# Attention over a cache on one core: row sums ahead of the values, the output weights spread around the last V blocks, and the result stored in halves

## The chip, the cores and the metric

The kernel runs on one core of a Trainium2 chip. The metric is the device time of one execution in microseconds (us). All durations that are read from a profile come from one profiled execution.

## The reference

Eight sequences of four tokens each (32 tokens) attend over a cache of 2048 keys and values. There are 32 query heads and 8 key/value heads of width 128, so four query heads share one key/value head.

```python
q = (x @ wq).reshape(B, Sq, Hq, Dh).transpose(0, 2, 1, 3)     # B=8, Sq=4, Hq=32, Dh=128
k = jnp.repeat(k_cache, 4, axis=1)                            # k_cache: (8, 8, 2048, 128) bf16
v = jnp.repeat(v_cache, 4, axis=1)
scores = jnp.einsum("bhqd,bhkd->bhqk", q, k) * (Dh ** -0.5)
p = softmax(scores, axis=-1)
o = jnp.einsum("bhqk,bhkd->bhqd", p, v)
return o.transpose(0, 2, 1, 3).reshape(B, Sq, Hq * Dh) @ wo   # wo: (4096, 512) bf16
```

The caches are 32 MB each, and wq and wo are 4 MB each.

## The kernel before

**Units and steps.** The work is cut into 32 units. A unit is one pair p of key/value heads (p = 0 to 3) of one sequence b (b = 0 to 7), with p as the outer index. Each unit has a K block and a V block of 1 MB each. Each unit is worked on in two half steps (hf = 0 and 1), so there are 64 half steps. The order of the instructions on each engine is the order in which the program writes them (a manual schedule), and the framework adds the waits.

**One pass of the main loop (L316).** The K side runs ahead of the V side. In the pass with number `step`, half step i = step + 7 has its K block transposed on TensorE (`transpose_part`, L199) and copied out of PSUM to `kt`. VectorE (DVE) makes three of four such copies (L206) and ScalarE (ACT) the one for the second part of the second half (L204). Half step j = step + 6 has its scores computed (L217), and ACT writes their exponentials to `probs` (L227). Half step `step` itself has its values computed (`values`, 16 matmuls at L241 into `o_ps`).

**Row sums.** `norms(u)` multiplies the exponentials of a whole unit by a matrix of ones, in two matmuls into `l_ps` (L255). DVE sums the result over 16 chunks (L263) and takes the reciprocal (L267). In the kernel before, this stands ahead of the values of the unit's second half. `finish(u)` multiplies the values by the reciprocals (L272) into `oT_all`, behind the values of the second half.

**Back to token rows.** When the 8 units of a pair p are finished, `to_tokens(p)` transposes its 8 heads into `nat` (L284), and DVE copies them to `nat_sb` (L290). `to_wo_rows(p)` transposes these again in another order into `perm` (L299), and DVE copies them to `oP[p]` (L304). The two run in the even passes of the next pair with b = 1 and b = 2, and for the last pair behind the loop. `l_ps`, `nat` and `perm` share one PSUM buffer (pool `psum_l`).

**The output projection.** `project(p, r0, n)` adds n matmuls of 512 columns to `out_ps` (L308), with a part of wo as the moving operand. All 32 matmuls of the kernel accumulate into this one tile of 32 x 512 fp32. Project(0) runs in the pass NH - 5 = 59, and the others run behind the loop.

**The loads.** All loads are issued by SyncE (SP) on one queue, in the order of the list `loads` (L114 to L121): K blocks run three units ahead of V blocks, with wo quarter 0 behind V29. A K block waits for one of 7 buffers and a V block for one of 6 (`load_ready`, L123). In the pass NH - 1 - 2 * VB = 51 the list is empty, and the remaining quarters of wo are issued, the last of them in three pieces (L339 to L343). The end of the order of loads is thus V29, wo 0, V30, V31, wo 1, wo 2, wo 3 (4 + 2 + 2 rows). wo takes the SBUF space of wq.

**The end.** DVE and ACT each copy half of `out_ps` to `out_sb`, and SP stores it (L356 to L358).

Of the kernel before, what the change touches and what calls it, by code (L numbers as in the profile page):

```python
# [8 lines left out]
BF16 = mybir.dt.bfloat16  # L9
# [5 lines left out]
def kernel(  # L15
# [9 lines left out]
    nc = tc.nc  # L25

    B, Sq, D = x.shape
# [4 lines left out]
    T = B * Sq  # L32
# [7 lines left out]
    NU = G2 * B  # L40
    NH = 2 * NU
# [4 lines left out]
    WR = HP  # L46
    DH = D // 2
# [5 lines left out]
    const = ctx.enter_context(tc.tile_pool(name="const", bufs=1))  # L53
# [20 lines left out]
    pick = const.tile([128, 2, 2, Dh // 2], BF16, name="pick")  # L74
    ident4 = const.tile([128, 128], FP32, name="ident4")
    oT_all = const.tile([128, Hq, B, Sq], BF16, name="oT_all")
    out_sb = const.tile([T, D], BF16, name="out_sb")
    oP = [const.tile([128, WR, T], BF16, name=f"oP{p}") for p in range(G2)]
    ident = const.tile([128, 128], BF16, name="ident")
    ones = const.tile([128, 128], BF16, name="ones")  # L80
# [26 lines left out]
    def load_wo(p, r0, n):  # L107
        rows = wo[p * HP * 128 : (p + 1) * HP * 128, :].rearrange("(q r) j -> q r j", r=WR)
        nc.sync.dma_start(wo_sb[:, p, r0 : r0 + n, :], rows[:, r0 : r0 + n, :])
# [3 lines left out]
    loads = []  # L113
    for u in range(NU + KA):  # L114
        if u < NU:
            loads.append(("k", u))
        if u >= KA - 1 and u - KA + 1 < NU:
            loads.append(("v", u - KA + 1))
        if u == NU:
            loads.append(("wo", 0))  # L120
    loads.reverse()  # L121

    def load_ready(nk, nv):  # L123
# [16 lines left out]
    for e in range(2):  # L140
        for g in range(2):
            nc.vector.tensor_copy(
                out=pick[:, e, g, :], in_=ident[:, :].rearrange("d (k e) -> d e k", e=2)[:, e, :]
# [12 lines left out]
    for p in range(G2):  # L156
        psq = psum_s.tile([128, HP, T], FP32, tag="s", name="psq")
        for h in range(HP):
# [10 lines left out]
            out=qT_all[:, p, :, :, :],  # L169
            in_=psq[:, :, :].rearrange("d h (b s) -> d b h s", b=B),  # L170
            mul=scale,
        )
    for p in range(G2):
# [9 lines left out]
        for g in range(2):  # L183
            rows = slice(g * 64, (g + 1) * 64)
            (nc.scalar.copy if g else nc.vector.tensor_copy)(  # L185
                out=q_bd[rows, p, :, :, g, :], in_=pse[rows, :, :, :]
# [5 lines left out]
    def transpose_part(i, part):  # L192
        u, hf = divmod(i, 2)
        c0 = hf * HC + part * (HC // 2)
        kp = psum_k.tile([128, HC // 4, 128], FP32, tag="k", name="kp")
        k4 = ks[u][:, :, :].rearrange("s c d -> s (c d)").bitcast(FP32)
        for j in range(HC // 4):
            w = (c0 // 2 + j) * 128
            nc.tensor.transpose(kp[:, j, :], k4[:, w : w + 128], ident4[:, :])  # L199
        kp2 = kp[:, :, :].rearrange("k j s -> k (j s)").bitcast(BF16)  # L200
        k_t = ktpool.tile([128, HC // 4, 128, 2], BF16, tag="kt", name="kt")
        kt2 = k_t[:, :, :, :].rearrange("k j s e -> k (j s e)")
        if part == 1 and hf == 1:
            nc.scalar.copy(out=kt2, in_=kp2)  # L204
        else:
            nc.vector.tensor_copy(out=kt2, in_=kp2)  # L206
        kt[(i, part)] = k_t

    def scores(i):
        u, hf = divmod(i, 2)  # L210
        p, b = units[u]
        pr = probs[u % len(probs)]
        s_ps = psum_s.tile([128, HC, NQ], FP32, tag="s", name="s_ps")
        for j in range(HC // 2):
            k_t = kt[(i, j // (HC // 4))]
            for e in range(2):
                nc.tensor.matmul(  # L217
                    s_ps[:, 2 * j : 2 * j + 2, :],
                    lhsT=k_t[:, j % (HC // 4), :, e],
                    rhs=q_bd[:, p, e, b, :, :],  # L220
                    start=(e == 0),
                    stop=(e == 1),
                )
        for g in range(2):
            rows = slice(g * 64, (g + 1) * 64)
            cols = slice(g * NQ // 2, (g + 1) * NQ // 2)
            nc.scalar.activation(  # L227
                out=pr[rows, hf * HC : (hf + 1) * HC, cols], in_=s_ps[rows, :, cols], func=EXP
            )
# [3 lines left out]
    def values(i):  # L233
        u, hf = divmod(i, 2)
        p, b = units[u]
        pr = probs[u % len(probs)]
        if hf == 0:
            o_ps[u] = psum_o.tile([128, NQ], FP32, tag="o", name="o_ps")
        for c in range(HC):
            cc = hf * HC + c  # L240
            nc.tensor.matmul(  # L241
                o_ps[u][:, :],
                lhsT=vs[u][:, cc, :],
                rhs=pr[:, cc, :],
                start=(cc == 0),
                stop=(cc == C - 1),
            )
# [3 lines left out]
    def norms(u):  # L251
        pr = probs[u % len(probs)]
        l_ps = psum_l.tile([128, LC, NQ], FP32, tag="l", name="l_ps")
        for c in range(0, C, LC):
            nc.tensor.matmul(  # L255
                l_ps[:, :, :],
                lhsT=ones[:, :],
                rhs=pr[:, c : c + LC, :],
                start=(c == 0),
                stop=(c + LC == C),  # L260
            )
        l_sb = small.tile([128, NQ], FP32, tag="l_sb", name="l_sb")
        nc.vector.tensor_reduce(  # L263
            out=l_sb[:, :], in_=l_ps[:, :, :].rearrange("d c q -> d q c"), axis=AX, op=ADD
        )
        r_sb = small.tile([128, NQ], FP32, tag="r_sb", name="r_sb")
        nc.vector.reciprocal(r_sb[:, :], l_sb[:, :])  # L267
        r_sbs[u] = r_sb

    def finish(u):  # L270
        p, b = units[u]
        nc.vector.tensor_tensor(  # L272
            out=oT_all[:, p * HP : (p + 1) * HP, b, :],
            in0=o_ps[u][:, :].rearrange("d (h s) -> d h s", h=HP),
            in1=r_sbs[u][:, :].rearrange("d (h s) -> d h s", h=HP),
            op=mybir.AluOpType.mult,
        )
# [3 lines left out]
    def to_tokens(p):  # L281
        nat = psum_l.tile([T, HP, 128], BF16, tag="l", name="nat")
        for h in range(HP):
            nc.tensor.transpose(  # L284
                nat[:, h, :],
                oT_all[:, p * HP + h, :, :].rearrange("d b s -> d (b s)"),
                ident[:, :],
            )
        nat_sb = small.tile([T, HP * 128 // WR, WR], BF16, tag="nat_sb", name="nat_sb")
        nc.vector.tensor_copy(  # L290
            out=nat_sb[:, :, :].rearrange("t q r -> t (q r)"),
            in_=nat[:, :, :].rearrange("t h d -> t (h d)"),
        )
        nats[p] = nat_sb

    def to_wo_rows(p):
        perm = psum_l.tile([128, WR, T], BF16, tag="l", name="perm")
        for r in range(WR):
            nc.tensor.transpose(  # L299
                perm[:, r, :],  # L300
                nats[p][:, :, :].rearrange("t q r -> t r q")[:, r, :],
                ident[:T, :T],
            )
        nc.vector.tensor_copy(out=oP[p][:, :, :], in_=perm[:, :, :])  # L304

    def project(p, r0, n):
        for r in range(r0, r0 + n):
            nc.tensor.matmul(  # L308
                out_ps[:, :],
                lhsT=oP[p][:, r, :],  # L310
                rhs=wo_sb[:, p, r, :],
                start=(p == 0 and r == 0),
                stop=(p == G2 - 1 and r == WR - 1),
            )

    for step in range(-L - 1, NH):  # L316
        i, j = step + L + 1, step + L
        if i < NH:
            transpose_part(i, 0)
        if 0 <= j < NH:  # L320
            scores(j)
        if i < NH:
            transpose_part(i, 1)
        u, hf = divmod(step, 2)
        if step >= 0:
            p, b = units[u]
            if hf == 1:
                norms(u)
            values(step)
            if hf == 1:  # L330
                finish(u)
            elif p > 0 and b == 1:
                to_tokens(p - 1)
            elif p > 0 and b == 2:
                to_wo_rows(p - 1)
        load_ready(min((i + 1) // 2, NU), max((step + 1) // 2, 0))
        if step == NH - 1 - 2 * VB:
            assert not loads
            load_wo(1, 0, WR)  # L339
            load_wo(2, 0, WR)  # L340
            load_wo(3, 0, 4)
            load_wo(3, 4, 2)
            load_wo(3, 6, 2)  # L343
        if step == NH - 5:
            out_ps = psum_s.tile([T, D], FP32, tag="s", name="out_ps")
            project(0, 0, WR)

    to_tokens(3)
    project(1, 0, 4)
    to_wo_rows(3)  # L350
    project(1, 4, 4)
    project(2, 0, WR)
    project(3, 0, 4)
    project(3, 4, 2)
    project(3, 6, 2)
    nc.vector.tensor_copy(out=out_sb[:, :DH], in_=out_ps[:, :DH])  # L356
    nc.scalar.copy(out=out_sb[:, DH:], in_=out_ps[:, DH:])  # L357
    nc.sync.dma_start(out=out.flatten_outer_dims(), in_=out_sb[:, :])  # L358


# [28 lines left out]
```

## Time and profile before

| | us |
|---|---|
| median of 6 runs | 193.42 |
| lowest and highest | 193.12, 194.64 |
| the profiled execution | 193.26 |
| its span on the core | 191.5 |

| engine | busy us (share of the span) |
|---|---|
| PE (TensorE matmul) | 153.6 (80%) |
| DVE (VectorE) | 112.5 (59%) |
| ACT (ScalarE) | 86.3 (45%) |
| queue of SP's loads | 95.3% of 16 DMA engines, 75.57 MB |

The profile's times count from the start of the span. PE is TensorE's matmuls, PEld its loads of weights, SPq the issuing of DMAs on SP. A row of the timeline gives the start, the duration from first to last, the engine, the line of the kernel, the operation, what it writes and reads, and how many instructions were merged; brackets give the idle time before it and what ended it. The chain of waits follows the work that ended last back to what released it at each step. TensorE's granted clock was at its full value throughout (1.0).

### The profile page before, as it was taken

Reading aid. Unit: us, or ns where it says so; the run is one execution under the profiler, and the core shown is the slowest. Engines: PE = TensorE matmul, PEld = TensorE weight load, DVE = VectorE, ACT = ScalarE, POOL = GpSimd, SP = SyncE. Lnnn points to the kernel's source line nnn. Section 1 sums busy time; section 2 is a strip of 40 time slices with the busy share of each in tenths; the row PEclk is TensorE's granted clock in tenths of the full one; section 3 lists DMA queues with packets and bytes.
Section 4 is the critical chain, followed back from the end, with each engine's and each line's share of the span. In section 5 each row is a group of like instructions: output and inputs, shape, how many; then the busy total and the mean of one; then the engine's idle time right before and its main releaser. Section 6 shows DMA issues by size and latency. Waiting matters only on the chain.

```text
span 191.5 us, 6364 instructions
## 1 busy us (share of the span) xinstructions
PE 153.6 (80%) x2830; PEld 136.0 (71%) x2860; DVE 112.5 (59%) x220; ACT 86.3 (45%) x170; POOL 1.1 (1%) x8
## 2 busy tenths in 40 slices
PE   0018977899999999999988889988885899889593
PEld 0016966788888888998888878877775788775451
DVE  6402754477776767777666667666663676665520
ACT  2004465655555555555554445444554455551000
POOL 2000000000000000000000000000000000000000
PEclk9999999999999999999999999999999999999999
DMA  6989999999999999999999999999999999999940
GB/s 226 438 368 430 419 426 414 419 423 418 418 419 419 418 419 418 421 419 414 428 412 421 421 414 424 414 423 416 421 416 423 418 423 418 412 428 414 401 170 7
DMA packets 10347, 75.97 MB, mean 397 GB/s; under 512 B 1168, under 2 KB 1232, under 8 KB 1616
## 3 DMA queue, kind: packets, MB, share of 16 engines
q1 hardware_dynamic: 10320, 75.57, 95.3%
q8 instruction: 22, 0.36, 0.8%
q14 instruction: 5, 0.04, 0.1%
HBM read 75.53 MB, written 0.03 MB: 395 GB/s over the span
## 4 chain that ended last, share of the span: by engine, by line
DMA 92%; PE 5%; DVE 1%; issue 0%; SPq 0%; ACT 0%; DVEq 0%
DMA k_sb<-in_k_cache_dram 64%; DMA v_sb<-in_v_cache_dram 21%; DMA wq_sb<-in_wq_dram 6%; PE out_ps L308 3%; PE kp L199 1%; PE o_ps L241 1%; PE l_ps L255 0%; DVE l_sb L263 0%; PE nat L284 0%; PE perm L299 0%; PE s_ps L217 0%; DVE out_sb L356 0%; SPq L111 0%; DVE r_sb L267 0%; ACT out_sb L357 0%
## 5 line engine op out<-in xcount | busy, mean ns | idle before, releaser
L206 DVE COPY kt<-kp 128x1024 bf16<-128x1024 bf16 x96 | 65.8, 688 | 44.8 <-PE kp L199 44.5
L199 PE MATMUL kp<-ident,k_sb 128*128 128x128 f32 x512 | 80.8, 284 | 10.1 <-DMA k_sb<-in_k_cache_dram 9.5
L227 ACT ACTIVATE probs<-s_ps 64x256 bf16<-64x256 f32 x128 | 48.4, 378 | 70.3 <-PE s_ps L217 69.5
L199 PEld LDWEIGHTS kp<-ident,k_sb 128*128 128x128 f32 x512 | 55.2, 143 | 11.7 <-issue 10.3
L217 PE MATMUL s_ps<-q_bd,kt 128*128 128x64 bf16 x1024 | 43.5, 193 | 6.7 <-ACT kt L204 6.0
L217 PEld LDWEIGHTS <-kt 128*128 128x128 bf16 x1024 | 39.6, 98 | 9.7 <-ACT kt L204 7.9
L241 PEld LDWEIGHTS <-v_sb 128*128 128x128 bf16 x1024 | 34.6, 96 | 10.0 <-DMA v_sb<-in_v_cache_dram 2.1
L241 PE MATMUL o_ps<-probs,v_sb 128*128 128x32 bf16 x1024 | 35.4, 176 | 1.7 <-DMA v_sb<-in_v_cache_dram 1.2
L204 ACT COPY kt<-kp 128x1024 bf16<-128x1024 bf16 x32 | 32.4, 1012 | 0.8
L263 DVE TENSOR_REDUCE l_sb<-l_ps 128x32 f32<-128x512 f32 x32 | 21.8, 682 | 5.0 <-remote 2.0
L255 PE MATMUL l_ps<-probs,ones 128*128 128x512 bf16 x34 | 12.6, 379 | 1.2
L267 DVE RECIPROCAL r_sb<-l_sb 128x32 f32<-128x32 f32 x32 | 11.3, 353 | 1.1
L185 DVE CAST q_bd<-pse 64x512 bf16<-64x512 f32 x4 | 2.6, 683 | 10.8 <-PE pse L176 10.8
L161 PE MATMUL psq<-xT_sb,wq_sb 128*128 128x32 bf16 x128 | 3.6, 188 | 6.3 <-DMA wq_sb<-in_wq_dram 6.3
L272 DVE TENSOR_TENSOR oT_all<-o_ps,r_sb 128x32 bf16<-128x32 f32 x32 | 6.1, 192 | 3.3
L161 PEld LDWEIGHTS <-wq_sb 128*128 128x128 bf16 x128 | 3.5, 104 | 6.4 <-DMA wq_sb<-in_wq_dram 6.4
L168 ACT ACTIVATE qT_all<-psq 128x256 bf16<-128x256 f32 x4 | 1.5, 386 | 14.0 <-PE psq L161 14.0
L308 PE MATMUL out_ps<-wo_sb,oP 128*32 128x512 bf16 x32 | 7.4, 380 | 0.0
L357 ACT CAST out_sb<-out_ps 32x256 bf16<-32x256 f32 x1 | 0.4, 362 | 15.3 <-DVE out_sb L356 15.3
L255 PEld LDWEIGHTS <-ones 128*128 128x128 bf16 x64 | 6.0, 98 | 0.4
L152 PE MATMUL xtp<-ident,x_sb 32*128 32x32 bf16 x4 | 0.5, 190 | 6.8 <-DVE xT_sb L155 4.3
L152 PEld LDWEIGHTS <-x_sb 32*128 32x128 bf16 x4 | 0.3, 112 | 6.8 <-issue 4.4
(23 smaller groups left out, 30.1 us busy)
## 6 DMA issues: line engine op xcount, KB each, us to landing
k_sb<-in_k_cache_dram SPq DMA_DIRECT2D x32, 1024.0 KB, 19.9
v_sb<-in_v_cache_dram SPq DMA_DIRECT2D x32, 1024.0 KB, 19.8
wq_sb<-in_wq_dram SPq DMA_DIRECT2D x1, 4096.0 KB, 12.4
wo_sb<-in_wo_dram SPq DMA_DIRECT2D x3, 1024.0 KB, 19.8
wo_sb<-in_wo_dram SPq DMA_DIRECT2D x1, 512.0 KB, 18.6
wo_sb<-in_wo_dram SPq DMA_DIRECT2D x2, 256.0 KB, 15.8
x_sb<-in_x_dram SPq DMA_DIRECT2D x1, 32.0 KB, 1.6
out_dram<-out_sb SPq DMA_DIRECT2D x1, 32.0 KB, 1.5
```

What stands on the lines that cost most here:

```text
L161: nc.tensor.matmul(psq[:, h, :], lhsT=wq_sb[:, r, hh * 128 : (hh + 1) * 128], rhs=xT_sb[:, r, :], start=(r == 0), stop=(r == R - 1),)
L199: nc.tensor.transpose(kp[:, j, :], k4[:, w : w + 128], ident4[:, :])
L204: nc.scalar.copy(out=kt2, in_=kp2)
L206: nc.vector.tensor_copy(out=kt2, in_=kp2)
L217: nc.tensor.matmul(s_ps[:, 2 * j : 2 * j + 2, :], lhsT=k_t[:, j % (HC // 4), :, e], rhs=q_bd[:, p, e, b, :, :], start=(e == 0), stop=(e == 1),
L227: nc.scalar.activation(out=pr[rows, hf * HC : (hf + 1) * HC, cols], in_=s_ps[rows, :, cols], func=EXP)
L241: nc.tensor.matmul(o_ps[u][:, :], lhsT=vs[u][:, cc, :], rhs=pr[:, cc, :], start=(cc == 0), stop=(cc == C - 1),)
L255: nc.tensor.matmul(l_ps[:, :, :], lhsT=ones[:, :], rhs=pr[:, c : c + LC, :], start=(c == 0), stop=(c + LC == C),)
L263: nc.vector.tensor_reduce(out=l_sb[:, :], in_=l_ps[:, :, :].rearrange("d c q -> d q c"), axis=AX, op=ADD)
L267: nc.vector.reciprocal(r_sb[:, :], l_sb[:, :])
L272: nc.vector.tensor_tensor(out=oT_all[:, p * HP : (p + 1) * HP, b, :], in0=o_ps[u][:, :].rearrange("d (h s) -> d h s", h=HP), in1=r_sbs[u][ ...
L308: nc.tensor.matmul(out_ps[:, :], lhsT=oP[p][:, r, :], rhs=wo_sb[:, p, r, :], start=(p == 0 and r == 0), stop=(p == G2 - 1 and r == WR - 1),)
```

## The change

Three things change. `norms(u)` moves from the unit's second half step to its first, ahead of the values of both halves. wo quarter 1 enters the list of loads behind V30, so the end of the order of loads becomes V29, wo 0, V30, wo 1, V31, wo 2, wo 3 in three pieces; project(1) moves into the pass NH - 3 = 61, behind the values of V30's second half. `out_sb` becomes two tiles of 256 columns, filled by DVE and ACT, and stored by a DMA of SP and one of ACT.

```diff
-    out_sb = const.tile([T, D], BF16, name="out_sb")
+    out_sb = [const.tile([T, DH], BF16, name=f"out_sb{i}") for i in range(2)]
...
-        if u == NU:
-            loads.append(("wo", 0))
+        if u in (NU, NU + 1):
+            loads.append(("wo", u - NU))
...
         if step >= 0:
             p, b = units[u]
-            if hf == 1:
+            if hf == 0:
                 norms(u)
             values(step)
...
         if step == NH - 1 - 2 * VB:
             assert not loads
-            load_wo(1, 0, WR)
             load_wo(2, 0, WR)
             load_wo(3, 0, 4)
             load_wo(3, 4, 2)
...
         if step == NH - 5:
             out_ps = psum_s.tile([T, D], FP32, tag="s", name="out_ps")
             project(0, 0, WR)
+        elif step == NH - 3:
+            project(1, 0, WR)
 
     to_tokens(3)
-    project(1, 0, 4)
     to_wo_rows(3)
-    project(1, 4, 4)
     project(2, 0, WR)
...
-    nc.vector.tensor_copy(out=out_sb[:, :DH], in_=out_ps[:, :DH])
-    nc.scalar.copy(out=out_sb[:, DH:], in_=out_ps[:, DH:])
-    nc.sync.dma_start(out=out.flatten_outer_dims(), in_=out_sb[:, :])
+    o2 = out.flatten_outer_dims()
+    nc.vector.tensor_copy(out=out_sb[0][:, :], in_=out_ps[:, :DH])
+    nc.scalar.copy(out=out_sb[1][:, :], in_=out_ps[:, DH:])
+    nc.sync.dma_start(out=o2[:, :DH], in_=out_sb[0][:, :])
+    nc.scalar.dma_start(out=o2[:, DH:], in_=out_sb[1][:, :])
```

## The prediction

> **What bounds the kernel now.** I read the page's chain of work first. DMA is 92% of it:
>
> ```profile
> DMA 92%; PE 5%; DVE 1%; issue 0%; SPq 0%; ACT 0%; DVEq 0%
> ```
>
> So until the last block lands, the engines follow the stream of loads. TensorE's own slack confirms it: in a middle step it sits 0.83 us before the K transposes, released by the load of K.
>
> ```profile
> 100.88 0.42 PEld L199 LDWEIGHTS kp<-ident,k_sb 128*128 128x128 f32 x4 [0.83 <-issue]
> 100.91 0.63 PE L199 MATMUL kp<-ident,k_sb 128*128 128x128 f32 x4 [0.76 <-DMA k_sb<-in_k_cache_dram]
> ```
>
> Next, the chain of waits in order of time, from 159 us on (start, duration, what):
>
> ```profile
> 159.45 19.78 DMA v_sb<-in_v_cache_dram
> 179.23 0.05 issue
> 179.28 0.57 PE o_ps L241 x16
> 179.84 0.45 PE l_ps L255 x2
> 180.30 0.02 issue
> 180.32 0.70 DVE l_sb L263
> 181.02 0.02 issue
> 181.04 0.36 DVE r_sb L267
> ...
> 181.50 0.20 DVE oT_all L272
> 181.70 0.04 issue
> 181.75 0.62 PE nat L284 x8
> 182.37 0.86 PE out_ps L308 x4
> 183.23 0.60 PE perm L299 x8
> 183.84 4.43 PE out_ps L308 x20
> ```
>
> After it come only the DVE copy (188.29 to 188.71), the ACT copy (188.74 to 189.10) and the store. From the landing of V31 at 179.23 to the last matmul at 188.27 is 9.04 us. The stream does not end there: three MB of wo follow. SP's own timeline gives each issue:
>
> ```profile
> 154.44 0.33 SPq L109 DMA_DIRECT2D wo_sb<-in_wo_dram  x1
> 156.98 2.80 SPq L102 DMA_DIRECT2D v_sb<-in_v_cache_dram  x2
> 161.89 10.25 SPq L109 DMA_DIRECT2D wo_sb<-in_wo_dram  x5
> 189.13 0.35 SPq L358 DMA_DIRECT2D out_dram<-out_sb  x1
> ```
>
> These are wo quarter 0, then V30 (156.98) and V31 (159.45), then quarters 1 to 3 in five pieces. Each MB lands 19.8 us after its issue, and issues are 2.47 us apart, since SP waits for a landing before each. So quarter 0 lands at 174.24, V30 at 176.76, V31 at 179.23, quarter 1 at 161.89 + 19.8 = 181.69. Taken issue by issue, the remaining pieces land at 184.2, 185.4, 186.0 and 186.7. TensorE reaches the first matmul on quarter 2 at 183.84 + 4 x 0.216 = 184.7 and on quarter 3 at 186.4. It waits for none: 20 matmuls in 4.43 us is an unbroken run. The end is therefore V31's landing plus TensorE's serial tail.
>
> [...] the ACT copy started 0.03 us after DVE's had ended. But both wrote one tile, out_sb[...]
>
> **The change, part by part**, against the profiled run (193.26 us, span 191.5, 1.76 around it; it lies 0.16 below the median of 193.42).
>
> 1. *wo.* Quarter 1 now leaves SP ahead of V31. Both are 1 MB in 8 KB runs, so the stream keeps its sizes and order and two labels change place: quarter 1 takes the landing at 179.23, V31 that at 181.69. **Cost +2.46 us** at the head of the tail. SP's 0.33 us of issue is only moved, and SP idles between issues. V31's buffer was free by 159.45, so it is at 161.89. Quarters 2 and 3 keep their landings.
>
> 2. *project(1) into the stream.* Its 8 matmuls now follow values(61). Quarter 1 is there at 179.23, so they run 179.28 to 181.01 in issue (8 x 0.216). They fill TensorE's wait for V31. This removes 8 matmuls from the tail, but not all at full price. The four between nat and perm took 0.86 us, and beside them ran DVE's copy of nat (0.68, plus 0.11 of handing over), on which perm waits anyway: saved 0.86 - 0.79 = 0.07. The four behind perm were bare: 4 x 0.216 = 0.87. **Together -0.94.**
>
> 3. *Row sums of unit 31.* Their 2 matmuls now stand behind project(1) and ahead of values(62). They finish at 181.01 + 0.60 = 181.61; DVE reduces until 182.33 (0.68 and 0.04) and takes reciprocals until 182.71 (0.36). Beside this values(62) and (63), with nothing between, run as 32 matmuls from 181.74. The row for such a pair is 0.95:
>
> ```profile
> 172.88 0.95 PE L241 MATMUL o_ps<-probs,v_sb 128*128 128x32 bf16 x32
> ```
>
> They end at 182.70, so both inputs of the multiply are ready at the same moment, and it starts at about 182.8 (0.1 us behind the reciprocal, as before) and ends at 183.0. From landing to there it was 2.47 us (181.70); it becomes 1.31. **Saved 1.16.** If quarter 1 came x later with V31 in place, x would be added here at once: project(1) heads TensorE's queue, and the sums and values(62) stand behind it.
>
> 4. *Row sums of the other units.* Two matmuls (0.60), a reduce (0.68) and a reciprocal (0.35) per unit move from odd steps to even ones. DVE has two kt copies of 0.69 in odd steps and one in even ones (ACT takes the other, L204), so its load gets more even. Where to_tokens and to_wo_rows run (even steps, b = 1, 2), nat and perm now wait in their one PSUM buffer for that step's reduce and hold up TensorE, with the next K transposes behind it, for up to 1 us, six times in all. The cover is the 0.8 us of waiting per unit and the loaded V blocks; the last such place is unit 26, five units ahead of the end. I take **0**; without the cover, at most 1 us.
>
> 5. *Tail.* nat 183.04 to 183.66, copy to 184.38, perm 184.45 to 185.05, then project(2) and (3), 16 matmuls: 4.43 - 4 x 0.216 = 3.57, end 188.62. Quarter 2 (184.2) and quarter 3 (185.4 on; used from 186.8) are in. The sum of the parts agrees: +2.46 - 0.94 - 1.16 = +0.36 on 188.27. I take **+0.4** for the tie in part 3.
>
> 6. *Copies and stores.* The trace shows neither ACT copying without DVE's out_sb ahead of it nor a store from ACT. Bounds for the copies: side by side, the later ends 0.42 after the matmuls where it was 0.83, so -0.4; in turn, 0. I take 0[...]. Then ACT's half leaves last, right behind its own copy, and DVE's half, sent 0.4 us sooner, gains nothing. Bounds for the half store: its 16 KB less, at some 420 GB/s, are 0.04 us; the first load of SP's queue (x, 32 KB) landed 1.6 us after issue against 1.5 for the store, and a second queue to await at the end may cost more. So -0.05 to +0.3; I take 0.
>
> Sum: +0.4 on the profiled run, 193.66; on the median, **193.8 us**.
>
> **Rivals.** About 0.5%, some 1.0 us, is what a measurement of this kernel can tell from no change.
>
> *A (0.5), the forecast:* what the tail loses in work it loses again by waiting for V31. 193.8, its own range 193.4 to 194.3.
>
> *B (0.2), the copies run side by side,* because only the shared out_sb held ACT: 193.8 - 0.4 = 193.4. For it: the wait view names out_sb. [...] This is no measurable change either.
>
> *C (0.17), slower: an added gap in the stream ahead of V31.* SP's issues, 2.5 us apart as a rule, have four gaps of 3.9 to 4.0 (18.5, 34.8, 82.0 and 140.6 us), each some 1.5 us more, while the core's bytes per second stay level[...]. Fetches of instructions share these engines (22 of 16 KB)[...]. One more such gap gives 193.8 + 1.5 = 195.3. It decides from an added 0.6 us on. Against it: instructions and transfers stay as many as they were, and five runs of six lie within 0.5 us.
>
> *D (0.08), one gap fewer:* 192.3, with the same evidence.
>
> *E (0.05), the change does not what it says:* if landings bunch so that quarter 1 comes with V31, project(1) and the sums are back in the tail at 8 x 0.216 + 0.6 = 2.3 us: 196. The landings of before, 2.47 apart, speak against it.
>
> **How the numbers follow.** Likeliest is A: 193.8. A and B lie within 0.5%, less a little of each end: 0.68. Slower: C with the upper ends of the store and of part 4, and part of E: 0.20. Faster: D and the low end of B: 0.12. The range runs from 192.7 (below B by its bounds, toward D) to 195.0 (A with the dear store and a stall, toward C).
>
> **What would show it.** In the changed profile: v_sb's last landing near 181.7; project(1)'s 8 matmuls at 179.3 to 181.2; 32 values matmuls in one run; no l_ps behind them in the chain; 16 matmuls of out_ps behind perm, ending near 188.6; the ACT copy behind DVE's or beside it. Wrong if V31 lands elsewhere than in quarter 1's old place, if out_ps waits for wo, or if the span changes in its middle.

## The result, and the profile after

| | before | after |
|---|---|---|
| median us (runs) | 193.51 (72) | 195.53 (35) |
| lowest, highest | 193.12, 196.04 | 193.66, 197.25 |
| profiled execution: time, span | 193.26, 191.5 | 196.11, 194.3 |
| its mean granted TensorE clock | 1.0 | 0.991 |

The comparison of runs gives a ratio of 1.0046, with a 95% interval of 1.0025 to 1.0067: slower by about 0.9 us, inside the range and just inside the 0.5% that was called no measurable change. It leaves out the runs over 1.5% above the fastest of their kernel, which are the 8 of the changed kernel's highest group. The medians of all runs are further apart (1.0104), and the changed kernel's, 195.53, lies above the upper end of the range, 195.0. That cannot be understood without one fact: the times of one kernel come in groups. The changed kernel has 11 executions from 193.66 to 194.06, 16 from 195.25 to 195.99 and 8 from 196.76 to 197.25. The kernel before has 42 of 72 from 193.12 to 193.60 and 30 from 194.49 on. Lowest against lowest, the change costs 0.54 us, where 0.4 was forecast. What the forecast did not have is how often the changed kernel leaves its lowest group: 24 of 35 executions, against 30 of 72 before.

The profiled execution of after is one of the longer ones. Its chain of waits from 159 us on (start, duration, what):

```profile
159.48 20.36 DMA wo_sb<-in_wo_dram
179.84 0.04 issue
179.88 1.89 PE out_ps L308 x8
181.77 0.55 PE l_ps L255 x2
182.32 0.02 issue
182.34 0.70 DVE l_sb L263
183.04 0.02 issue
183.07 0.36 DVE r_sb L267
...
183.53 0.20 DVE oT_all L272
...
183.77 0.64 PE nat L284 x8
...
184.43 0.69 DVE nat_sb L290
185.12 0.05 issue
185.16 0.67 PE perm L299 x8
185.84 5.26 PE out_ps L308 x16
```

The order is the forecast one, step for step: quarter 1 lands, project(1) runs, the row sums follow, then nat, perm and 16 matmuls. The chain runs through quarter 1, project(1) and the sums rather than through V31: the values of V31, which landed at 182.3, were ready at 183.3, and the reciprocals only 0.1 us later. One number does not fit: **16 matmuls took 5.26 us**, not 3.57. The table by stage shows why. Its columns are the stage, its length, the busy time (and count) of PE, PEld, DVE, ACT and POOL, the granted TensorE clock, DMA share and GB/s:

```profile
182.00:184.00 2.00, 1.50 (x38) 1.10 (x37) 1.24 (x3) 0.00 (x0) 0.00 (x0) 1.00 0.56 222
184.00:186.00 2.00, 1.23 (x17) 0.90 (x14) 0.81 (x2) 0.00 (x0) 0.00 (x0) 0.99 0.41 161
186.00:188.00 2.00, 2.00 (x6) 0.76 (x5) 0.16 (x1) 0.00 (x0) 0.00 (x0) 0.50 0.06 25
188.00:190.00 2.00, 2.00 (x7) 0.74 (x6) 0.00 (x0) 0.00 (x0) 0.00 (x0) 0.66 0.00 0
```

At 186 us TensorE's clock is 0.50, and it comes back before 190. In that stretch TensorE's loads of weights, one for each matmul, start 0.43 us apart (186.44, 186.87, 187.29, ...) where the unbroken run of before gave 0.216. Eight matmuls at half clock cost 8 x 0.21 = 1.7 us, just the difference of 5.26 and 3.57. By the two stages, 0.50 over 2 us and 0.66 over the next 2 are 2.0 + 0.68 x 2 = 3.4 us at half clock. The longest wait of TensorE in this tail was 1.52 us (ahead of project(1)). What lowers the clock, the views do not show.

The waits ahead of nat and perm, and the end, in the timeline of after (in brackets the idle time before the row, and what ended it):

```profile
183.77 0.62 PE L284 MATMUL nat<-ident,oT_all 128*32 128x128 bf16 x8 [0.44 <-DVE oT_all L272]
184.43 0.68 DVE L290 COPY nat_sb<-nat 32x1024 bf16<-32x1024 bf16 x1 [0.71 <-PE nat L284]
185.16 0.67 PE L299 MATMUL perm<-ident,nat_sb 32*128 32x32 bf16 x8 [0.77 <-DVE nat_sb L290]
...
191.12 0.41 DVE L356 CAST out_sb<-out_ps 32x256 bf16<-32x256 f32 x1 [4.95 <-PE out_ps L308]
191.56 0.35 SPq L358 DMA_DIRECT2D out_dram<-out_sb  x1
191.56 0.36 ACT L357 CAST out_sb<-out_ps 32x256 bf16<-32x256 f32 x1 [18.50 <-DVE out_sb L356]
191.95 0.38 ACTq L359 DMA_DIRECT2D out_dram<-out_sb  x1
```

Before perm TensorE now idles for 0.77 us. In the kernel before, four matmuls of project(1) stood there, and they had looked nearly free to move. The last four rows show the copies one behind the other, although the two no longer write one tile of SBUF.

### The profile page after: what moved, and what is told of

Its sections match the earlier page's. It is cut to its first block, busy times and chain, and to the rows that moved or that the text cites. A ratio compares the mean times of both kernels' runs of the same rounds, so it can differ in the third digit from the quotient of the medians.

```text
span 194.3 us, 6365 instructions
## 1 busy us (share of the span) xinstructions
PE 153.1 (79%) x2830; PEld 135.4 (70%) x2860; DVE 113.8 (59%) x220; ACT 86.3 (44%) x170; POOL 1.1 (1%) x8
## 4 chain that ended last, share of the span: by engine, by line
DMA 91%; PE 6%; DVE 1%; issue 0%; SPq 0%; ACT 0%; DVEq 0%
DMA k_sb<-in_k_cache_dram 63%; DMA v_sb<-in_v_cache_dram 11%; DMA wo_sb<-in_wo_dram 10%; DMA wq_sb<-in_wq_dram 7%; PE out_ps L308 4%; PE kp L199 1%; DVE l_sb L263 0%; DVE nat_sb L290 0%; PE perm L299 0%; PE nat L284 0%; PE l_ps L255 0%; PE s_ps L217 0%; DVE out_sb L356 0%; PE o_ps L241 0%; SPq L111 0%
## 5 line engine op out<-in xcount | busy, mean ns | idle before, releaser
L199 PE MATMUL kp<-ident,k_sb 128*128 128x128 f32 x512 | 79.6, 281 | 12.3 <-DMA k_sb<-in_k_cache_dram 12.2
L199 PEld LDWEIGHTS kp<-ident,k_sb 128*128 128x128 f32 x512 | 54.0, 141 | 14.0 <-issue 13.3
L217 PE MATMUL s_ps<-q_bd,kt 128*128 128x64 bf16 x1024 | 42.1, 193 | 3.4 <-ACT kt L204 2.6
L308 PE MATMUL out_ps<-wo_sb,oP 128*32 128x512 bf16 x32 | 9.1, 443 | 2.5 <-DMA wo_sb<-in_wo_dram 2.5
L308 PEld LDWEIGHTS <-oP 128*32 128x32 bf16 x32 | 3.4, 109 | 6.9 <-issue 4.7
## 6 DMA issues: line engine op xcount, KB each, us to landing
k_sb<-in_k_cache_dram SPq DMA_DIRECT2D x32, 1024.0 KB, 20.3
wo_sb<-in_wo_dram SPq DMA_DIRECT2D x3, 1024.0 KB, 20.3
```

What stands on the lines that cost most here:

```text
L217: nc.tensor.matmul(s_ps[:, 2 * j : 2 * j + 2, :], lhsT=k_t[:, j % (HC // 4), :, e], rhs=q_bd[:, p, e, b, :, :], start=(e == 0), stop=(e == 1),
L308: nc.tensor.matmul(out_ps[:, :], lhsT=oP[p][:, r, :], rhs=wo_sb[:, p, r, :], start=(p == 0 and r == 0), stop=(p == G2 - 1 and r == WR - 1),)
```

## The experiments

Three theories are named in the expectations. P is the prediction's arithmetic: V31's landing plus TensorE's serial tail. C adds that TensorE falls to half clock when it has too little to do between the last V blocks. R blames the stream of loads or the second store queue instead. Results are given as lowest and median time, and as the share of executions over 1 us above the kernel's own lowest. The kernel before ran beside each group of experiments: lowest 193.24, 193.23 and 193.22, medians 193.49, 193.55 and 194.57 in the groups E1 to E4, E5 to E8 and E9 to E11. Differences of lowest times are taken within a group. The changed kernel was not run again beside them; where a run is compared with it, the comparison is across groups.

### E1: only the row sums ahead

```diff
-            if hf == 1:
+            if hf == 0:
                 norms(u)
```

> Only the row sums are ahead of the values; wo, copies and store as before. Theory P (the end is V31's landing plus TensorE's serial tail): V31 still lands near 179.2, the multiply ends near 180.5 instead of 181.7, then project(1) waits for wo quarter 1 (181.7), so the last matmul ends near 187.6 instead of 188.3: 0.6 to 0.7 us less than before at full clock, 192.7. Theory C (TensorE falls to half clock when it has too little to do between the last V blocks): many executions lose 1.5 to 3 us of that again. Rival R (the excess comes from the stream of loads or the second store queue, not from the clock): 192.7 throughout.

Lowest 192.83 (-0.41), median 194.14, 13 of 22 executions over 1 us above the lowest, ratio 0.9998 (0.9964 to 1.0032). The profile is of one at 192.94, at full clock:

```profile
180.39 0.19 DVE L272 TENSOR_TENSOR oT_all<-o_ps,r_sb 128x32 bf16<-128x32 f32 x1 [0.96 <-PE o_ps L241]
...
181.87 1.02 PE L308 MATMUL out_ps<-wo_sb,oP 128*32 128x512 bf16 x4 [0.62 <-DMA wo_sb<-in_wo_dram]
```

The multiply starts at 180.4, 1.1 us earlier than before, and project(1) then waits 0.62 us for quarter 1. So the sums ahead are a gain at full clock, and the gain is lost in more than half of the executions. The gain is smaller than P had it (0.41 us for 0.6 to 0.7): quarter 1 landed at 181.83, and the four matmuls behind it took 1.02 us. Both P, but for this size, and C hold; R does not, as there is neither a new stream nor a new queue.

### E2: only wo quarter 1 ahead of V31 and project(1) between

```diff
-        if u == NU:
-            loads.append(("wo", 0))
+        if u in (NU, NU + 1):
+            loads.append(("wo", u - NU))
...
-            load_wo(1, 0, WR)
...
+        elif step == NH - 3:
+            project(1, 0, WR)
...
-    project(1, 0, 4)
     to_wo_rows(3)
-    project(1, 4, 4)
```

> Only wo quarter 1 ahead of V31 and project(1) between; row sums, copies and store as before. P: +2.46 for V31's landing, -0.94 for project(1) out of the tail: +1.5 us, 194.9 at full clock, V31's landing near 181.7. C: some executions with half clock behind V31 on top (+1.6). R: if the quarter in front of V31 costs nothing, no change.

Lowest 194.82 (+1.58), median 196.42, 13 of 22 over 1 us above, ratio 1.0096 (1.0065 to 1.0127). The profile is of one at 196.62, and its chain has V31's load:

```profile
161.88 19.91 DMA v_sb<-in_v_cache_dram
...
186.38 5.26 PE out_ps L308 x16
```

V31 lands at 181.79, quarter 1's old place. P's +1.5 is met, and so is C: the 16 matmuls take 5.26 us here too, at a granted clock of 0.77, 0.50 and 0.87 in the stretches of 2 us from 186 us on.

### E3: only the store in halves

```diff
-    out_sb = const.tile([T, D], BF16, name="out_sb")
+    out_sb = [const.tile([T, DH], BF16, name=f"out_sb{i}") for i in range(2)]
...
-    nc.sync.dma_start(out=out.flatten_outer_dims(), in_=out_sb[:, :])
+    nc.sync.dma_start(out=o2[:, :DH], in_=out_sb[0][:, :])
+    nc.scalar.dma_start(out=o2[:, DH:], in_=out_sb[1][:, :])
```

> Only out_sb in two tiles and the store in two halves. P: the ACT copy still waits for DVE's [...], so 0 to +0.3 us, 193.4 to 193.6. If the copies ran side by side: 193.0. R (the second queue is what costs): +0.5 us or more. C: nothing of the clock changes.

Lowest 193.32 (+0.08), median 193.56, 6 of 14 over 1 us above, as often as the kernel before; ratio 0.9985 (0.995 to 1.0021). The second queue costs nothing that counts. The profiled execution was a long one, 195.3, and shows that the tail of before, which E3 keeps, can lose its clock too (by stage, columns as above):

```profile
182.00:184.00 2.00, 1.59 (x11) 1.04 (x12) 0.92 (x3) 0.00 (x0) 0.00 (x0) 0.65 0.57 227
184.00:186.00 2.00, 2.00 (x13) 0.85 (x12) 0.30 (x2) 0.00 (x0) 0.00 (x0) 0.50 0.42 167
186.00:188.00 2.00, 2.00 (x11) 0.93 (x10) 0.00 (x0) 0.00 (x0) 0.00 (x0) 0.99 0.05 17
```

### E4: three matmuls held back for the gap

```diff
-            project(1, 0, WR)
+            project(1, 0, 5)
...
     to_tokens(3)
+    project(1, 5, 3)
     to_wo_rows(3)
```

> The changed kernel, with the last 3 of project(1)'s 8 matmuls held back and put between the transposes of nat and perm, beside DVE's copy. P: same time as the changed kernel at full clock (193.9), since that gap is 0.77 us and 3 matmuls take 0.65. C: the gap's idle time helps to bring the clock down, so executions with a half-clock tail (two in three of the changed kernel) get clearly fewer and the median falls toward 194. R: the spread of the times stays that of the changed kernel, median near 195.5.

Lowest 193.67 (+0.43), **median 193.88**, highest 194.71; 2 of 22 over 1 us above; ratio 0.9992 (0.9966 to 1.0017). No work is added and none taken away. Three of the matmuls that the change took out of the gap go back to it, and the groups from 195.2 on are gone. The tail of the profile runs as forecast, at full clock (timeline):

```profile
183.51 0.81 PE L308 MATMUL out_ps<-wo_sb,oP 128*32 128x512 bf16 x3
...
184.45 0.66 PE L299 MATMUL perm<-ident,nat_sb 32*128 32x32 bf16 x8
185.03 3.63 PE L308 MATMUL out_ps<-wo_sb,oP 128*32 128x512 bf16 x16
```

The last matmul ends at 188.67, where the prediction's sum has 188.62. The mean clock of this execution is 0.991 all the same. Half clock lies in the middle of the stream, from 146 to 152 us (0.83, 0.50 and 0.82 in three stretches of 2 us), and V31 still left SP at 161.86, so it cost no time there.

### E5: E4 with out_ps in two tiles

```diff
-            out_ps = psum_s.tile([T, D], FP32, tag="s", name="out_ps")
+            out_ps = [psum_s.tile([T, DH], FP32, tag="s", name=f"out_ps{i}") for i in range(2)]
...
-            nc.tensor.matmul(
-                out_ps[:, :],
+            for i in range(2):
+                nc.tensor.matmul(
+                    out_ps[i][:, :],
...
-                rhs=wo_sb[:, p, r, :],
+                    rhs=wo_sb[:, p, r, i * DH : (i + 1) * DH],
```

> The kernel with three matmuls held back, and out_ps as two PSUM tiles of 256 columns in two banks (64 matmuls of 256 columns for 32 of 512). P: the ACT copy no longer waits for DVE's, both start behind the last matmul: 0.4 us less than with three held back, lowest near 193.3, if 64 half matmuls take as long as 32 whole ones. Against it: ACT still starts behind DVE[...]: 193.7. C and R: nothing else changes.

Lowest 193.32 (+0.09, against +0.43 for E4), median 193.42, 2 of 14 over 1 us above, ratio 0.9987 (0.996 to 1.0013). In the timeline the copies now lie side by side, and ACT is released by TensorE:

```profile
188.80 0.41 DVE L358 CAST out_sb<-out_ps 32x256 bf16<-32x256 f32 x1 [3.20 <-PE out_ps L309]
188.90 0.36 ACT L359 CAST out_sb<-out_ps 32x256 bf16<-32x256 f32 x1 [15.74 <-PE out_ps L309]
```

So it was the shared out_ps that kept ACT behind DVE: the two copies start 0.10 us apart here and 0.44 us apart in E4 (188.70 and 189.14). The expectations call the two tiles two banks. No view shows where in PSUM a tile lies, so whether the wait went by the tile or by its place was not shown.

### E6: the changed kernel kept busy

`keep_warm(n)` issues n matmuls of 128 x 512 into a PSUM tile that nothing reads.

```diff
+            keep_warm(6)
             project(1, 0, WR)
...
+    keep_warm(1)
     to_tokens(3)
+    keep_warm(2)
     to_wo_rows(3)
```

> The changed kernel with 9 added matmuls of 512 columns, into a tile that nothing reads, in TensorE's waits: 6 behind the values of V30, 1 ahead of nat, 2 between nat and perm. P: they lie in waits, so nothing at full clock: 193.8 as the changed kernel's lowest executions. C: TensorE stays busy, the half-clock tail goes: nearly all executions within 0.7 us of the lowest, median near 194, against 195.5 for the changed kernel. R: median stays near 195.5, or grows by the added work.

Lowest 193.71 (+0.48), median 193.92, highest 194.33; 0 of 14 over 1 us above; ratio 1.0002 (0.9979 to 1.0025). Added work brings the median down by 1.6 us from the changed kernel's 195.53. Only C foresees that.

### E7: the kernel before with its gap bare

```diff
-    project(1, 0, 4)
     to_wo_rows(3)
-    project(1, 4, 4)
+    project(1, 0, WR)
```

> The kernel before, with the 4 matmuls of project(1) between nat and perm put behind perm with the other 4: the gap is left bare. P: the 4 matmuls leave the cover of DVE's copy, +0.8 us at full clock: lowest near 194.0. C: a bare gap in the tail brings the clock down more often or for more of the tail, so that the share of executions more than 1 us above the lowest grows from one third to more than half, and the median is 195 or more. R: the share stays one third, median near 194.2.

Lowest 195.81, median 197.02, ratio 1.017 (1.0132 to 1.0209), of 6 runs. None is near 194.0. Timeline of the profiled one, at 195.81, the lowest:

```profile
183.77 7.04 PE L308 MATMUL out_ps<-wo_sb,oP 128*32 128x512 bf16 x24
```

The granted clock was 0.56 from 184 to 186 us and 0.59 from 186 to 188. At full clock 24 matmuls take 23 x 0.216 + 0.38 = 5.35 us (0.38 is what one took in the profile of before). Without the other 1.69 us the time would be 194.1, as P has it. This is the sharpest of the tests: the kernel before, its loads, sums and store untouched, loses 2.6 us in its lowest time by one gap, of which 1.7 are clock. That the other five executions, at 196.35 to 197.73, lost their clock too is inferred from their times; they were not profiled.

### E8: the sums ahead, nothing else of the change's order, and TensorE kept busy

On E1, with E5's two tiles and the halves:

```diff
+            if step == NH - 2:
+                keep_warm(4)
             values(step)
...
     to_tokens(3)
+    keep_warm(2)
     project(1, 0, 4)
```

> Row sums ahead, the order of loads of before (wo quarter 1 behind V31), two banks for out_ps and the store in halves, and 6 added matmuls in TensorE's waits (4 ahead of V31's values, 2 between nat and perm), whose result nothing reads. P: the lowest executions of the kernel with only the row sums ahead (192.8) less 0.4 for the copies side by side: 192.4. C: with TensorE kept busy nearly all executions lie within 0.8 us of that, median 192.6, under the kernel before. R: a spread up to 195 remains.

Lowest 192.46 (-0.77), median 192.94, 6 of 22 over 1 us above, ratio 0.9954 (0.9934 to 0.9975): faster than both kernels. All 22 spans lie between 190.7 and 191.2. The six long executions have 2.7 to 2.9 us around the span in place of some 1.8, which makes their times 193.57 to 193.80; where that comes from stays open.

### E9: the same with work of the kernel's own

```diff
-            project(0, 0, WR)
+            project(0, 0, 2)
...
+            if step == NH - 2:
+                project(0, 2, 4)
             values(step)
...
     to_tokens(3)
-    project(1, 0, 4)
+    project(0, 6, 2)
+    project(1, 0, 3)
     to_wo_rows(3)
-    project(1, 4, 4)
+    project(1, 3, 5)
```

> As the kernel with the row sums ahead, the order of loads of before, two banks and halves, but TensorE's waits are filled with work of its own in place of added matmuls: 2 of project(0)'s rows run at pass 59, 4 ahead of V31's values, 2 with 3 rows of project(1) between nat and perm. P: 192.5 at full clock, as the version with added matmuls. C: the clock holds where the filled waits hold it, median 192.5 to 193.0; since two fewer matmuls of filling are there and pass 59 has 6 rows fewer, a part of the executions may still fall to half clock (1.3 us more). R: spread up to 195 as with the row sums alone.

Lowest 192.41 (-0.81), **median 192.79**, highest 193.69, 5 of 22 over 1 us above, ratio 0.9938 (0.9916 to 0.996). It needs no wasted work: project(0), whose weights are there early, is spread over the waits.

### E10 and E11: which wait must be filled

E10 has only the `keep_warm(6)` of E6, ahead of project(1), and E11 only the `keep_warm(2)` between nat and perm.

> The changed kernel with only the 6 added matmuls behind the values of V30 (the wait for wo quarter 1); the gap between nat and perm stays bare. C, with the early wait as what brings the clock down: median near 194. C, with the late gap: spread and median stay near 195.5. R: 195.5.

> The changed kernel with only 2 added matmuls between nat and perm; the wait for wo quarter 1 stays bare. C, with the late gap as what brings the clock down: median near 194, as with three held back. C, with the early wait: near 195.5. R: 195.5.

E10: lowest 193.76, median 195.44, 12 of 22 over 1 us above, ratio 1.0037 (1.0009 to 1.0065). E11: lowest 193.79, median 193.95, 5 of 14 above, ratio 1.0009 (0.9978 to 1.0041). The medians go the way of the late gap, but 12 of 22 against 5 of 14 is too little to part the two by these runs alone; that the late gap carries most of it rests on E4 and E7, which fill or bare that gap and put nothing into the earlier waits. The 1.5 us wait for quarter 1 is twice as long as the gap, and filling it leaves the share of long executions near the changed kernel's 24 of 35. It is not without effect: the group above 196.7, 8 of 35 in the changed kernel, is missing from E10's 22 executions as from E11's 14. The long executions that E11 still has are gone only where the early wait is filled too (E6, with one more matmul ahead of nat) or where the gap's filling is three matmuls (E4).

## Why the prediction was right, and where not

1. *wo ahead of V31, +2.46.* Right. V31 took quarter 1's place (E2: 181.79; E4: 161.86 + 19.90 = 181.76). In the profile of after it came at 182.3, because loads took 20.3 us in that execution in place of 19.8; it left SP at 162.00, 0.1 us behind quarter 1's old place.
2. *project(1), -0.94.* Right at full clock: E4's tail ends within 0.05 us of the sum. The step that failed stands here too: the four matmuls in the gap were priced as "saved 0.07", as if idle time of TensorE beside DVE's copy cost nothing. E7 prices the bare gap: 1.7 us of clock. One of the prediction's signs of being wrong, out_ps waiting for wo, is there in a form that costs nothing by itself: in the profile of after project(0) waits 1.02 us for quarter 0 and project(1) 1.52 us for quarter 1, both ahead of V31, and the tail waits for no quarter.
3. *Row sums, -1.16.* Right in size: E1's multiply starts 1.1 us sooner. The tie that was forecast is there, in the profile of after: values end at 183.3, reciprocals at 183.4.
4. *Middle steps, 0.* Right: nat and perm waited 1.2 us each for reduces, over three places each, and the end of the stream shows nothing of it (E4 issued V31 at 161.86, the kernel before quarter 1 at 161.89). The bound of 1 us per place was too wide; the trace has 0.4.
5. *The 16 matmuls of the tail, 3.57 us.* **The mis-sized term.** In longer executions they take 5.26 (profiles of after, E2 and E10). The clock was full in the profile of before and was taken as given; the prediction named no rival that lowers it. Of the kernel before, too, 30 of 72 runs are of the longer kind. Six times before the change were shown, and one of them, 194.64, was such a one.
6. *Copies in turn and half stores, 0.* Right, though the profile of before did not show what made ACT wait, and the 0 was the author's estimate. ACT starts 0.03 us behind DVE's end in after, and E3 costs 0.08 us. Rival B was wrong, and E5 says what it would have needed. Both half stores landed 1.4 us after their issue.

Rivals C and D (a gap in the stream more or less) can't explain the groups: E4, E6 and E7 move the share of long executions without touching a load. C's 195.3 lies close to the middle group by luck only; its cause is another. C's evidence is also one gap short: at 34.8 us SP had waited 2.1 us for a landing and then 1.5 us for TensorE's values to free a V buffer, so that only three of the four gaps are late landings.

So the measured 1.0046 is made of two parts: +0.54 us of path, near the 0.4 forecast, and a more frequent half clock. The range was made for a stall of the stream or a dear store, not for this, so that the number fell inside it is partly luck. No execution of the highest group (196.76 to 197.25) was profiled. By an estimate from the spacings of 0.43 and 0.216 us, all 16 matmuls at half clock would cost 16 x 0.21 = 3.4 us, near its distance of 3.1 us from the lowest group.

## What to carry to other kernels

Idle time of TensorE was not free in this tail, for its clock fell to 0.50 in some executions: here, where TensorE's last matmuls are the path, the three matmuls that fill its wait just ahead of them (0.65 us, E4) were worth 1.6 us of the median. Move work out of such a gap only with something to put in its place, best the kernel's own work whose data came early. And look at the spread of the times before pricing a tail from one profile at full clock. The mean clock of an execution does not tell, only where in the trace it is low: 0.982 stands beside 193.71 in E4 and beside 195.48 in the changed kernel.

## What the runs showed that was not expected

No single wait of TensorE in the profiled tails was longer than some 1.5 us, and a gap of 0.77 us decided how often the tail lost its clock (3.4 us at half clock in the profile of after; 1.4 + 2.0 = 3.4 by the stages of E3's). Filling it with three matmuls (0.65 us) took the share of executions over 1 us above the lowest from 24 of 35 to 2 of 22. The half clock in these tails came without a longer wait. How much work over how long a time keeps the clock up was not measured, nor why some executions of the same kernel fall to half clock in the tail and others do not.
